# Moving small products to GpSimd and filling TensorE with unread products in a fused attention and gated-MLP kernel

## The chip, the core and the metric

The kernel runs on one core of one Trainium2 chip. A core has five engines that run at the same time and wait for one another by semaphores: TensorE (in the profile PE, with its weight loads as PEld), VectorE (DVE), ScalarE (ACT), GpSimd (POOL) and SyncE (SP). SBUF is the memory that all of them read; PSUM holds what TensorE writes, in eight banks of 128 x 512 fp32. The metric is the device time of one execution in microseconds.

## What is computed

The input x is 2048 positions by 512. Branch A is attention with 32 heads of width 16 that share one key and one value head; branch B is a gated MLP with a product over positions; a sigmoid gate mixes them.

```python
g = sigmoid((x * gate_w).sum(-1, keepdims=True))
# branch A: q has 32 heads, k and v have one
q, k, v = x @ wq, x @ wk, x @ wv
p = softmax(einsum('bhqd,bkd->bhqk', q, k) * Dh ** (-0.5))
a = einsum('bhqk,bkd->bhqd', p, v)  -> heads side by side -> @ wo
# branch B
z = gelu(x @ w_in);  z1 = z[..., :688];  z2 = layernorm(z[..., 688:])
b = (z1 * (w_sp @ z2 + b_sp)) @ w_out
out = g * a + (1 - g) * b
```

The softmax has 32 x 2048 x 2048 exponentials; they are the largest part of the work.

## The kernel before

All instructions of all engines are laid out by a Python program when the kernel is built. It keeps a clock for TensorE, ScalarE and VectorE, and for the engine whose clock is earliest it picks the ready candidate with the smallest priority number; each candidate carries an estimated length in nanoseconds. The estimates set only the order of the instructions on each engine; on the chip, semaphores set the times.

A **block** is 128 keys by 512 queries of one head. A **unit** is 64 such blocks: 16 key tiles for a group of four heads, which lie in the four quarters of the TensorE array. There are 32 units. Scores of a block are one matmul (32 rows of the array). ScalarE takes scores from two PSUM areas of three and two banks in turn and writes exponentials P; VectorE takes some blocks from bank 5 (BD) and builds the exponential as a polynomial, twice squared, in X, in batches of four blocks. How many blocks VectorE gets is decided by the clocks of the layout.

```python
BD = 5; BO = 6; BM = 7            # PSUM banks: VectorE's scores, attention sum, everything else
EB = ((0, 3), (3, 2))             # ScalarE's score areas
C512, C344 = 218.0, 148.0         # estimated lengths, ns
C4, C2 = 40 + 0.26 * 256 * DB, 30 + 0.5208 * 256 * DB     # DB = 4

def exp_op(k, n):                                          # L548, ScalarE
    op("act", lambda a: a.activation(P[:, k % NP, 0:512 * n], ps[:, 512 * b0:512 * (b0 + n)], ACT.Exp), ...)
def d_A(m, i):                                             # L572, VectorE, "dA"
    op("dve", lambda v: v.tensor_scalar(X[:, m % NX, 512 * i:512 * i + 512], bank(BD), PA, PB, ALU.mult, ALU.add), ...)
def d_poly(m):      # L580 square, L582 add a constant, L584 square; each on two halves of 1024
    ... v.tensor_tensor(x, x, x, ALU.mult)                 # estimate C2
    ... v.tensor_scalar(x, x, PC, None, ALU.add)           # estimate C4
    ... v.tensor_tensor(p_, x, x, ALU.mult)                # estimate C2
```

P and X are multiplied with V by quarter-array matmuls into bank 6 (BO); a column of ones in V gives the softmax sum. When a unit is done, VectorE normalises it and transposes it into OT for the output projection:

```python
def norm(pgx, u):
    ... v.transpose(T1[:], bank(BO))                                     # L594
    ... v.reciprocal(rc[:].unsqueeze(2), t1[:, :, 16:17])                # L595
    ... v.tensor_tensor(rcg[:], rc[:], RHO[:, c, :], ALU.mult)           # L597, RHO: the gate
    ... v.tensor_tensor(Tn[...], t1[:, :, 0:16], rr[:]..., ALU.mult)     # L598
    if jj == 1:                                                          # every second unit
        ... v.transpose(OT[:, c, jp, :], Tn[:, pr, :])                   # L602
```

Everything else of TensorE (projections of x to K, Q, V, z1, z2, the product over positions, the output) runs as "groups" through bank 7 (BM): a list of pieces, then an evacuation by VectorE. Between two pieces of a group other work may be put. The squares of Q, 16 instructions (L342), serve a bound on the scores. Such a group of pieces is that of V, 16 small matmuls, each a piece:

```python
return Group("V%d" % c, [(70, piece(k, dt)) for k in range(4) for dt in range(4)], [(150, e1), (100, e2), (130, e3)], ...)
```

Where TensorE has nothing ready in the next 100 ns, the layout may put an **unread product**: a full-array matmul of ones with ones, whose result nobody reads. It does so when the load of the last 3400 ns, in full matmuls of 512 columns, is below KEEP. An unread product goes to bank BM and only while no group is in it:

```python
def keep_pick(now):
    while load and load[0][0] < now - 3400:
        load.popleft()
    if sum(w_ for _, w_ in load) >= KEEP or misc["cur"] is not None or misc["free"] + LAT > now or tl_state[12] or st_["pu"] >= NU:
        return None
    ...
    return (now, 9, C512 + sw("M"), emit, None, "M")
```

`tl_state[12]` is set when the output tile 12 has begun to be built in BM ahead of the end.

In the trace all full-array matmuls carry line 277 and all quarter-array ones line 278, because one helper emits them.

Of the kernel before, what the change touches and what calls it, by code (L numbers as in the profile page):

```python
# [43 lines left out]
KEEP = 6.5  # L44
# [103 lines left out]
def build_kernel(nc, x_d, wq_d, wk_d, wv_d, wo_d, win_d, wsp_d, bsp_d, wout_d, gw_d, out_d):  # L148
    es = ExitStack()
    with es:  # L150
# [53 lines left out]
        s01 = sb("s01", [128, 2], F32)  # L204
        ct = sb("ct", [128, 3, NMAX * 32], F32)
# [11 lines left out]
        nhalf = sb("nhalf", [128, NST], F32)  # L217
        rstd = sb("rstd", [128, NST], F32)
# [14 lines left out]
        op("pool", lambda g: g.memset(nhalf[:], -0.5), w=["nhalf"])  # L233
        op("pool", lambda g: g.memset(bspz[:], 0.0), w=["bspz"])
# [57 lines left out]
        C4, C2 = 40 + 0.26 * 256 * DB, 30 + 0.5208 * 256 * DB  # L292
# [34 lines left out]
        def g_K(c):  # L327
            def done(t):
                T[("K", 0, c)] = t
                if c == 3:  # L330
                    k_shift()
                    T["K1"] = t + 8000
            return Group("K%d" % c, [(C512, lambda dt=dt: k_mm(c, dt, BM)) for dt in range(4)], [(620, lambda: k_ev(c, BM))],
                         lambda: when(("x", c)), done)
# [6 lines left out]
        def q_sq(qt):  # L341
            dve_q.append((350, lambda: op("dve", lambda v: v.tensor_tensor(sq[:, qt % 4, :], QA[:, qt % NQ, :], QA[:, qt % NQ, :], ALU.mult),  # L342
                                          r=[("Q", qt % NQ)], w=[("sq", qt % 4)], tag="sq"), T["now"] + 800, setT(("sq", qt))))

        def g_Q(qt):
            def done(t):
# [3 lines left out]
                         [(620, lambda: op("dve", lambda v: v.tensor_copy(QA[:, qt % NQ, :], bank(BM)), r=[BMK], w=[("Q", qt % NQ)], tag="Qev"))],  # L350
                         lambda: when(("x", qt // 4), "wq1", *([("Udone", 2 * (qt - NQ) + 1)] if qt >= NQ else [])), done)

        def g_N(c):
# [7 lines left out]
            return Group("N%d" % c, [(C512 if j == 0 else 60.0, piece(j)) for j in range(4)], [(620, ev)],  # L361
# [20 lines left out]
        def g_V(c):  # L382
# [17 lines left out]
            return Group("V%d" % c, [(70, piece(k, dt)) for k in range(4) for dt in range(4)], [(150, e1), (100, e2), (130, e3)],  # L400
# [14 lines left out]
        def g_MC():  # L415
# [17 lines left out]
            return Group("MC", pieces, [(1950, e1), (320, e2), (320, e3), (320, e4), (250, e5), (320, e6)],  # L433
                         lambda: when(("Kt", 2), ("Kt", 3), ("V", 2), ("V", 3)), setT("MC"))

        def g_R(c):
            def piece(dt):
                return lambda: mm(bank(BM), gw_rep[:, dt, :], xT[:, dt, 512 * c:512 * c + 512], dt == 0, dt == 3, ["gwr", ("x", c)], [BMK], tag="R")
            cr = ct[:, :, :].rearrange("p a n -> p (a n)")[:, 0:512]
            ev = lambda: op("dve", lambda v: v.transpose(cr, bank(BM)), r=[BMK], w=["ct0", "ct1"], tag="Rt")  # L440

            def done(t):
                def f():
                    op("act", lambda a: a.activation(RHO[:, c, :].unsqueeze(2), cr.rearrange("p (b w) -> p b w", w=32)[:, :, 0:1], ACT.Exp),
                       r=["ct0", "ct1"], w=[("RHO", c)], tag="rho")
                    T[("RHO", c)] = T["now"] + 500
                act_q.append((250, f, t))
            return Group("R%d" % c, [(C512, lambda dt=dt: piece(dt)()) for dt in range(4)], [(660, ev)],
                         lambda: when(("x", c), "MC", *([("RHO", c - 1)] if c else [])), done)

        def g_z1(ft, tc):
# [4 lines left out]
            return Group("z1", [(C512, piece(dt)) for dt in range(4)], [(620, ev)], lambda: when("win", ("x", tc)), setT(("z1", ft, tc)))  # L456

        def g_z2(st, h):
# [5 lines left out]
            return Group("z2", [(C344, piece(dt)) for dt in range(4)], [(440, ev)], lambda: when("win", ("x", st // 4)), setT(("z2", st, h)))  # L464

        def gelu_ops():
            out = []
            for k in range(4):
                def f(k=k):
# [3 lines left out]
                    for i in range(4):  # L473
                        st = 4 * k + i
                        for h in range(2):
                            dve_q.append((440, lambda st=st, h=h: op("dve", lambda v: v.bn_stats(bst[:, st, h, :], z2[:, FH * st + 344 * h:FH * st + 344 * h + 344]),  # L476
                                                                     r=[("z2", st)], w=[("bst", st)], tag="bn"), t, None))
                        dve_q.append((150, lambda st=st: op("dve", lambda v: v.bn_aggr(mv[:, st, :], bst[:, st, :, :]), r=[("bst", st)], w=["mv"], tag="bn"), t, None))
# [108 lines left out]
        def norm(pgx, u):  # L587
# [141 lines left out]
        def pe_pick(now):  # L729
# [414 lines left out]
        for u in range(NU):  # L1144
# [39 lines left out]
            for c_, f_, t_ in norm(ps2, u):  # L1184
                f_()
# [90 lines left out]
```

## Time and profile before

| | before |
|---|---|
| time, median of 3 runs | 856.54 us (855.01 to 858.22) |
| span of the profiled execution | 851.2 us |
| PE busy | 789.3 us, 5416 matmuls |
| DVE busy | 765.5 us |
| ACT busy | 776.0 us, of it 749.6 in 647 exponentials |
| POOL busy | 10.9 us, 17 instructions |
| mean granted TensorE clock | 0.927 |
| blocks of VectorE ("dA") | 432 of 2048 |
| unread products | 81 (12 of them ahead of the first work) |

Busy shares are averages over stages that are unlike: in the first 35 us the input arrives; from 280 to 320 us ScalarE computes the GELU and VectorE the layer norm; from 834 us on only the last tiles are left. The granted clock is that at which TensorE was allowed to run, 1.00 being full speed. A group's line gives count, busy time, the mean length of one, and the idle time of its engine just before it with what ended it. Lengths of neighbours on VectorE overlap a little, so a sum of lengths is more than the busy time.

### The profile page before, as it was taken

To read this page: it belongs to the slowest core of one execution; us is meant where nothing else is said; L and a number is where in the kernel's file an instruction comes from. 1 tells how busy PE (TensorE), PEld (TensorE's weight loads), DVE (VectorE), ACT (ScalarE), POOL (GpSimd) and SP (SyncE) were. 2 spreads that over 40 slices of the span, in tenths; PEclk is the share of its full clock that TensorE was granted. 3 is DMA by queue.
4 is the path that set the end of the run, shared out by engine and by line. 5 is a ranking of instruction groups with operands and counts; after the bars stand their busy time and mean duration, and the time that the engine had idled before them with its cause. 6 is when DMAs were issued, how large, how long until landed. Compare 5 with 4: busy or idle time off the path is not lost.

```text
span 851.2 us, 13946 instructions
## 1 busy us (share of the span) xinstructions
PE 789.3 (93%) x5416; PEld 209.9 (25%) x5416; DVE 765.5 (90%) x1471; ACT 776.0 (91%) x668; POOL 10.9 (1%) x17
## 2 busy tenths in 40 slices
PE   8899899999998879999999999999999999998886
PEld 2212222222222112222222222222222222222212
DVE  3579998899999899999999998999998999998981
ACT  5879997899999988999999999999998999999992
POOL 2000000000000010000000000000000000000000
PEclk8759996899999889999999999999998999999757
DMA  9700000000000000001300003100013000000000
GB/s 218 144 0 2 1 1 1 1 1 1 1 1 1 2 0 2 1 1 26 87 13 2 1 1 82 44 1 2 2 31 76 20 1 2 1 1 1 1 1 28
DMA packets 49050, 17.00 MB, mean 20 GB/s; under 512 B 44129, under 2 KB 48913, under 8 KB 48978
## 3 DMA queue, kind: packets, MB, share of 16 engines
q1 hardware_dynamic: 46210, 15.23, 8.0%
q10 hardware_dynamic: 2640, 0.56, 0.4%
q8 instruction: 44, 0.72, 0.4%
q0 software_dynamic: 128, 0.26, 0.2%
q14 instruction: 28, 0.23, 0.1%
HBM read 3.20 MB, written 2.10 MB: 6 GB/s over the span
## 4 chain that ended last, share of the span: by engine, by line
DVE 54%; PE 34%; issue 7%; ACT 3%; DMA 2%; SPq 0%; ACTq 0%
PE ps L278 22%; DVE X L572 20%; PE ps L277 12%; DVE X L580 9%; DVE X L584 7%; DVE X L582 5%; ACT P L548 2%; DVE T L594 2%; DVE bst L476 2%; DVE z L455 1%; DMA KA<-KA 1%; DVE Tn L598 1%; DVE z L462 1%; DMA xT<-in_A_x_dram 1%; DVE z L509 1%
## 5 line engine op out<-in xcount | busy, mean ns | idle before, releaser
L548 ACT ACTIVATE P<-ps 128x1536 bf16<-128x1536 f32 (+1 forms) x647 | 749.6, 1244 | 52.3 <-PE ps L278 48.1
L278 PE MATMUL ps<-QA,KA 32*128 32x512 bf16 x2048 | 364.1, 406 | 33.6 <-DVE X L572 16.4
L572 DVE TENSOR_SCALAR X<-ps 128x512 f16<-128x512 f32 x432 | 294.3, 681 | 39.4 <-PE ps L278 38.1
L278 PE MATMUL ps<-P,V 128*32 128x512 bf16 x1616 | 168.7, 412 | 0.0
L278 PEld LDWEIGHTS ps<-QA,KA 32*128 32x128 bf16 x2048 | 87.8, 91 | 326.4 <-ACT P L548 128.9
L584 DVE TENSOR_TENSOR X<-X 128x1024 bf16<-128x1024 f16 x216 | 144.1, 680 | 0.0
L580 DVE TENSOR_TENSOR X<-X 128x1024 f16<-128x1024 f16 x216 | 141.9, 680 | 0.0
L277 PE MATMUL ps<-wT,z 128*128 128x512 bf16 x384 | 118.6, 384 | 0.0
L582 DVE TENSOR_SCALAR X<-X 128x1024 f16<-128x1024 f16 x216 | 84.0, 415 | 0.0
L278 PE MATMUL ps<-X,V 128*32 128x512 bf16 x432 | 71.4, 407 | 0.1
L278 PEld LDWEIGHTS ps<-P,V 128*32 128x32 bf16 x1616 | 33.7, 95 | 61.3 <-issue 57.8
L277 PEld LDWEIGHTS ps<-wT,z 128*128 128x128 bf16 x384 | 29.3, 97 | 62.2 <-issue 52.7
L277 PE MATMUL ps<-ones 128*128 128x512 bf16 x81 | 32.4, 487 | 8.2 <-DVE bst L476 5.1
L277 PE MATMUL ps<-win,xT 128*128 128x344 bf16 x128 | 33.4, 339 | 3.9 <-DVE z L462 2.6
L277 PE MATMUL ps<-xT,win 128*128 128x512 bf16 x96 | 31.3, 386 | 2.6 <-DVE z L455 2.1
L277 PE MATMUL ps<-wout,z 128*128 128x512 bf16 x96 | 31.5, 400 | 1.8 <-DVE outsb L534 1.4
L594 DVE STREAM_TRANSPOSE T<-ps 128x512 f32<-128x512 f32 x32 | 22.6, 705 | 7.2 <-PE ps L278 7.2
L277 PE MATMUL ps<-xT,wq 128*128 128x512 bf16 x64 | 23.0, 414 | 0.3 <-DVE z L509 0.2
L278 PEld LDWEIGHTS ps<-X,V 128*32 128x32 bf16 x432 | 17.1, 95 | 19.8 <-issue 12.8
L277 PE MATMUL ps<-wo,OT 128*128 128x512 bf16 x64 | 20.5, 393 | 0.0
L462 DVE CAST z<-ps 128x344 bf16<-128x344 f32 x32 | 16.1, 504 | 2.0 <-PE ps L277 2.0
L277 PEld LDWEIGHTS ps<-win,xT 128*128 128x128 bf16 x128 | 10.1, 100 | 29.5 <-issue 12.9
(97 smaller groups left out, 293.3 us busy)
## 6 DMA issues: line engine op xcount, KB each, us to landing
out_dram<-outsb SPq DMA_DIRECT2D x16, 128.0 KB, 1.7
win<-in_B_w_in_dram SPq DMA_DIRECT2D x2, 688.0 KB, 5.5
wout<-in_B_w_out_dram SPq DMA_DIRECT2D x1, 640.0 KB, 9.0
wo<-in_A_wo_dram SPq DMA_DIRECT2D x1, 512.0 KB, 6.6
wq<-in_A_wq_dram ACTq DMA_DIRECT2D x1, 384.0 KB, 8.4
wT<-in_B_w_sp_dram SPq DMA_TRANSPOSE x16, 4.4
KA<-KA POOLq DMA_DIRECT2D x4, 64.0 KB, 2.5
wq<-in_A_wq_dram ACTq DMA_DIRECT2D x1, 128.0 KB, 3.9
```

The source lines that it names most:

```text
L277: return t.matmul(dst, lhsT, rhs, start=start, stop=stop)
L278: return t.matmul(dst, lhsT, rhs, start=start, stop=stop, tile_position=tp)
L455: ev = lambda: op("dve", lambda v: v.tensor_copy(z1[:, ft, 512 * tc:512 * tc + 512], bank(BM)), r=[BMK], w=[("z1", ft)], tag="z1ev")
L462: ev = lambda: op("dve", lambda v: v.tensor_copy(z2[:, FH * st + 344 * h:FH * st + 344 * h + 344], bank(BM, 344)), r=[BMK], w=[("z2", st)] ...
L476: dve_q.append((440, lambda st=st, h=h: op("dve", lambda v: v.bn_stats(bst[:, st, h, :], z2[:, FH * st + 344 * h:FH * st + 344 * h + 344]) ...
L509: ev = lambda: op("dve", lambda v: v.tensor_tensor(dst, ps[0:n, 512 * BM:512 * BM + 512], dst, ALU.mult), r=[BMK, ("z1", ft)], w=[("u", ft ...
L548: op("act", lambda a: a.activation(P[:, k % NP, 0:512 * n], ps[:, 512 * b0:512 * (b0 + n)], ACT.Exp), r=[("sc", k % 2)], w=[("P", k % NP)] ...
L572: op("dve", lambda v: v.tensor_scalar(X[:, m % NX, 512 * i:512 * i + 512], bank(BD), PA, PB, ALU.mult, ALU.add), r=[("bk", BD)], w=[("X", ...
L580: res.append((C2, lambda x=x, k=k: op("dve", lambda v: v.tensor_tensor(x, x, x, ALU.mult), r=[k], w=[k], tag="dU")))
L582: res.append((C4, lambda x=x, k=k: op("dve", lambda v: v.tensor_scalar(x, x, PC, None, ALU.add), r=[k], w=[k], tag="dV")))
L584: res.append((C2, lambda x=x, k=k, p_=p_, kp=kp: op("dve", lambda v: v.tensor_tensor(p_, x, x, ALU.mult), r=[k], w=[kp], tag="dW")))
L594: res = [(660, lambda: o("dve", lambda v: v.transpose(T1[:], bank(BO)), r=[("bk", BO)], w=["T1"], tag="T1"), setT(("O", u)))]
```

## The change

Several things are changed together:

- The reciprocal, the product with the gate and the scaling of each unit but the last go from VectorE to GpSimd. GpSimd builds the reciprocal as a power of -1. The second transpose on VectorE is planned 6 us after the unit's end.
- The squares of Q go to GpSimd.
- The 16 matmuls of a V group are one piece; the 14 of the MC group (sums over key tiles that correct for what the polynomial leaves out) are two. The gate's groups R get a buffer of their own (`cr`) and no longer wait for MC; R(0) is ahead of it.
- Unread products: KEEP is 7.5; below LOW = 6.0 they have priority 1.5, ahead of the products with V (2) and of groups (3), and need no idle time; they may use bank BD when VectorE has no block in it.
- The estimated lengths are replaced by others taken from measured lengths.

The diff, cut to its core (`...` marks cuts; declarations, the clean-up of the slow path's call and a few estimates of evacuations from 620 to 600 are left out):

```diff
@@ -41,7 +41,8 @@
-KEEP = 6.5
+KEEP = 7.5
+LOW = 6.0
 ...
@@ -231,6 +234,7 @@
+        op("pool", lambda g: g.memset(mone[:], -1.0), w=["mone"])
 ...
@@ -289,7 +293,7 @@
-        C4, C2 = 40 + 0.26 * 256 * DB, 30 + 0.5208 * 256 * DB
+        C4, C2 = 68 + 0.26 * 256 * DB, 68 + 0.5208 * 256 * DB
 ...
@@ -339,15 +343,16 @@
         def q_sq(qt):
-            dve_q.append((350, lambda: op("dve", lambda v: v.tensor_tensor(sq[:, qt % 4, :], QA[:, qt % NQ, :], QA[:, qt % NQ, :], ALU.mult),
-                                          r=[("Q", qt % NQ)], w=[("sq", qt % 4)], tag="sq"), T["now"] + 800, setT(("sq", qt))))
+            op("pool", lambda g: g.tensor_tensor(sq[:, qt % 4, :], QA[:, qt % NQ, :], QA[:, qt % NQ, :], ALU.mult),
+               r=[("Q", qt % NQ)], w=[("sq", qt % 4)], tag="sq")
+            T[("sq", qt)] = T["now"] + 5000
 ...
             return Group("Q%d" % qt, [(C512, lambda dt=dt: q_mm(qt, dt, BM)) for dt in range(4)],
-                         [(620, lambda: op("dve", lambda v: v.tensor_copy(QA[:, qt % NQ, :], bank(BM)), r=[BMK], w=[("Q", qt % NQ)], tag="Qev"))],
+                         [(600, lambda: op("dve", lambda v: v.tensor_copy(QA[:, qt % NQ, :], bank(BM)), r=[BMK], w=[("Q", qt % NQ)], tag="Qev"))],
 ...
@@ -397,7 +402,11 @@
-            return Group("V%d" % c, [(70, piece(k, dt)) for k in range(4) for dt in range(4)], [(150, e1), (100, e2), (130, e3)],
+            def all_():
+                for k in range(4):
+                    for dt in range(4):
+                        piece(k, dt)()
+            return Group("V%d" % c, [(480, all_)], [(150, e1), (100, e2), (130, e3)],
 ...
@@ -430,30 +439,32 @@
             e6 = lambda: op("dve", lambda v: v.scalar_tensor_tensor(cc, cc, s01[:, 0:1], ct[:, 1, :], ALU.mult, ALU.add), r=["CC", "ct1", "s01"], w=["CC"], tag="CC")
-            return Group("MC", pieces, [(1950, e1), (320, e2), (320, e3), (320, e4), (250, e5), (320, e6)],
+            def some(h):
+                for c_, f_ in pieces[NMAX * h:NMAX * h + NMAX]:
+                    f_()
+            return Group("MC", [(500, lambda: some(0)), (500, lambda: some(1))], [(1950, e1), (320, e2), (320, e3), (320, e4), (250, e5), (320, e6)],
 ...
                 return lambda: mm(bank(BM), gw_rep[:, dt, :], xT[:, dt, 512 * c:512 * c + 512], dt == 0, dt == 3, ["gwr", ("x", c)], [BMK], tag="R")
-            cr = ct[:, :, :].rearrange("p a n -> p (a n)")[:, 0:512]
-            ev = lambda: op("dve", lambda v: v.transpose(cr, bank(BM)), r=[BMK], w=["ct0", "ct1"], tag="Rt")
+            ev = lambda: op("dve", lambda v: v.transpose(cr[:], bank(BM)), r=[BMK], w=["cr"], tag="Rt")
 ...
                 def f():
-                    op("act", lambda a: a.activation(RHO[:, c, :].unsqueeze(2), cr.rearrange("p (b w) -> p b w", w=32)[:, :, 0:1], ACT.Exp),
-                       r=["ct0", "ct1"], w=[("RHO", c)], tag="rho")
+                    op("act", lambda a: a.activation(RHO[:, c, :].unsqueeze(2), cr[:, :].rearrange("p (b w) -> p b w", w=32)[:, :, 0:1], ACT.Exp),
+                       r=["cr"], w=[("RHO", c)], tag="rho")
 ...
             return Group("R%d" % c, [(C512, lambda dt=dt: piece(dt)()) for dt in range(4)], [(660, ev)],
-                         lambda: when(("x", c), "MC", *([("RHO", c - 1)] if c else [])), done)
+                         lambda: when(("x", c), *([("RHO", c - 1)] if c else [])), done)
 ...
             ev = lambda: op("dve", lambda v: v.tensor_copy(z1[:, ft, 512 * tc:512 * tc + 512], bank(BM)), r=[BMK], w=[("z1", ft)], tag="z1ev")
-            return Group("z1", [(C512, piece(dt)) for dt in range(4)], [(620, ev)], lambda: when("win", ("x", tc)), setT(("z1", ft, tc)))
+            return Group("z1", [(C512, piece(dt)) for dt in range(4)], [(600, ev)], lambda: when("win", ("x", tc)), setT(("z1", ft, tc)))
 ...
@@ -473,9 +484,9 @@
-                            dve_q.append((440, lambda st=st, h=h: op("dve", lambda v: v.bn_stats(bst[:, st, h, :], z2[:, FH * st + 344 * h:FH * st + 344 * h + 344]),
+                            dve_q.append((520, lambda st=st, h=h: op("dve", lambda v: v.bn_stats(bst[:, st, h, :], z2[:, FH * st + 344 * h:FH * st + 344 * h + 344]),
 ...
-                        dve_q.append((150, lambda st=st: op("dve", lambda v: v.bn_aggr(mv[:, st, :], bst[:, st, :, :]), r=[("bst", st)], w=["mv"], tag="bn"), t, None))
+                        dve_q.append((135, lambda st=st: op("dve", lambda v: v.bn_aggr(mv[:, st, :], bst[:, st, :, :]), r=[("bst", st)], w=["mv"], tag="bn"), t, None))
 ...
@@ -588,19 +599,45 @@
-            fast = pgx is pg
 ...
-            rr = rcg if fast else rc
-            res = [(660, lambda: o("dve", lambda v: v.transpose(T1[:], bank(BO)), r=[("bk", BO)], w=["T1"], tag="T1"), setT(("O", u)))]
-            res.append((210, lambda: o("dve", lambda v: v.reciprocal(rc[:].unsqueeze(2), t1[:, :, 16:17]), r=["T1"], w=["rc"], tag="rc"), None))
-            if fast:
-                res.append((110, lambda: o("dve", lambda v: v.tensor_tensor(rcg[:], rc[:], RHO[:, c, :], ALU.mult), r=["rc", ("RHO", c)], w=["rcg"], tag="rcg"), None))
-            res.append((380, lambda: o("dve", lambda v: v.tensor_tensor(
-                Tn[:, pr, :].rearrange("p (b w) -> p b w", w=32)[:, :, 16 * jj:16 * jj + 16],
-                t1[:, :, 0:16], rr[:].unsqueeze(2).broadcast_to([128, 16, 16]), ALU.mult), r=["T1", "rcg" if fast else "rc"], w=[("Tn", pr, jj)], tag="Tn"), None))
-            if jj == 1:
-                res.append((650, lambda: o("dve", lambda v: v.transpose(OT[:, c, jp, :], Tn[:, pr, :]), r=[("Tn", pr, 0), ("Tn", pr, 1)], w=[("OT", c, jp)], tag="T2"),
-                            setT(("OT", c, jp))))
+            lsum = t1[:, :, 16:17]
+            tn = Tn[:, pr, :].rearrange("p (b w) -> p b w", w=32)[:, :, 16 * jj:16 * jj + 16]
+
+            def f_t1():
+                o("dve", lambda v: v.transpose(T1[:], bank(BO)), r=[("bk", BO)], w=["T1"], tag="T1")
+
+            def f_rc(e):
+                if e == "dve":
+                    o("dve", lambda v: v.reciprocal(rc[:].unsqueeze(2), lsum), r=["T1"], w=["rc"], tag="rc")
+                else:
+                    o("pool", lambda g: g.tensor_tensor(rc[:].unsqueeze(2), lsum, mone[:].unsqueeze(2), ALU.pow), r=["T1", "mone"], w=["rc"], tag="rc")
+
+            def f_rcg(e):
+                o(e, lambda v: v.tensor_tensor(rcg[:], rc[:], RHO[:, c, :], ALU.mult), r=["rc", ("RHO", c)], w=["rcg"], tag="rcg")
+
+            def f_tn(e, s_, k):
+                o(e, lambda v: v.tensor_tensor(tn, t1[:, :, 0:16], s_[:].unsqueeze(2).broadcast_to([128, 16, 16]), ALU.mult), r=["T1", k], w=[("Tn", pr, jj)], tag="Tn")
+
+            def f_t2():
+                o("dve", lambda v: v.transpose(OT[:, c, jp, :], Tn[:, pr, :]), r=[("Tn", pr, 0), ("Tn", pr, 1)], w=[("OT", c, jp)], tag="T2")
+
+            if pgx is not pg:
+                return [f_t1, lambda: f_rc("dve"), lambda: f_tn("dve", rc, "rc")] + ([f_t2] if jj else [])
+            res = []
+            if u < NU - 1:
+                def f_all():
+                    f_t1()
+                    f_rc("pool")
+                    f_rcg("pool")
+                    f_tn("pool", rcg, "rcg")
+                res.append((716, f_all, setT(("O", u)), 0.0))
+            else:
+                res.append((716, f_t1, setT(("O", u)), 0.0))
+                res.append((281, lambda: f_rc("dve"), None, 0.0))
+                res.append((205, lambda: f_rcg("dve"), None, 0.0))
+                res.append((387, lambda: f_tn("dve", rcg, "rcg"), None, 0.0))
+            if jj:
+                res.append((633, f_t2, setT(("OT", c, jp)), 6000.0 if u < NU - 1 else 0.0))
 ...
@@ -636,7 +673,7 @@
-        first = deque([g_V(0), g_K(1), g_K(2), g_V(1), g_K(3), g_V(2), g_V(3), g_MC(), g_R(0), g_Q(1), g_R(1), g_R(2), g_R(3)])
+        first = deque([g_V(0), g_K(1), g_K(2), g_V(1), g_K(3), g_V(2), g_V(3), g_R(0), g_MC(), g_Q(1), g_R(1), g_R(2), g_R(3)])
 ...
@@ -884,9 +921,12 @@
             if not cands or min(c[0] for c in cands) > now + 100:
-                tl = tail_pick(now) or keep_pick(now)
+                tl = tail_pick(now)
 ...
                     cands.append(tl)
+            kp = keep_pick(now)
+            if kp and (kp[1] < 9 or not cands or min(c[0] for c in cands) > now + 100):
+                cands.append(kp)
 ...
@@ -897,13 +937,20 @@
                 load.popleft()
-            if sum(w_ for _, w_ in load) >= KEEP or misc["cur"] is not None or misc["free"] + LAT > now or tl_state[12] or st_["pu"] >= NU:
+            have = sum(w_ for _, w_ in load)
+            if have >= KEEP or st_["pu"] >= NU:
+                return None
+            if misc["cur"] is None and misc["free"] + LAT <= now and not tl_state[12]:
+                b = BM
+            elif dbank["blk"] is None and dbank["free"] + LAT <= now and not tl_state[13]:
+                b = BD
+            else:
 ...
                 after = [pg.ops["dve"][-1]] if gel_on and gel else []
-                mm(bank(BM), ones[:, 0:128], ones[:], True, True, ["ones"], [BMK], tag="keep", after=after)
-            return (now, 9, C512 + sw("M"), emit, None, "M")
+                mm(bank(b), ones[:, 0:128], ones[:], True, True, ["ones"], [("bk", b)], tag="keep", after=after)
+            return (now, 1.5 if have < LOW else 9, C512 + sw("M"), emit, None, "M")
 ...
@@ -938,8 +985,8 @@
-                for z, (c_, f_, d_) in enumerate(norm(pg, u)):
-                    norm_q.append((c_, f_, (lambda u=u: when(("RHO", u // 8))) if z == 2 else t_end + LAT, d_))
+                for c_, f_, d_, w_ in norm(pg, u):
+                    norm_q.append((c_, f_, lambda w_=w_: None if when(("RHO", u // 8)) is None else t_end + LAT + w_, d_))
 ...
@@ -997,7 +1044,7 @@
-                    cands.append((t, 1, 94 + 426.7 * len(bl), e2, f2))
+                    cands.append((t, 1, (0, 510, 940, 1346)[len(bl)], e2, f2))
 ...
@@ -1033,7 +1080,7 @@
-                cands.append((dbank["ready"], 3, 600, e1, f1))
+                cands.append((dbank["ready"], 3, 601, e1, f1))
 ...
```

More of the change, by code (lines that the diff above doesn't have):

```diff
@@ L204, in build_kernel @@
         s01 = sb("s01", [128, 2], F32)
+        cr = sb("cr", [128, 512], F32)
         ct = sb("ct", [128, 3, NMAX * 32], F32)
@@ L217, in build_kernel @@
         nhalf = sb("nhalf", [128, NST], F32)
+        mone = sb("mone", [128, NST], F32)
         rstd = sb("rstd", [128, NST], F32)
@@ L332, in done @@
                     T["K1"] = t + 8000
-            return Group("K%d" % c, [(C512, lambda dt=dt: k_mm(c, dt, BM)) for dt in range(4)], [(620, lambda: k_ev(c, BM))],
+            return Group("K%d" % c, [(C512, lambda dt=dt: k_mm(c, dt, BM)) for dt in range(4)], [(600, lambda: k_ev(c, BM))],
                          lambda: when(("x", c)), done)
@@ L360, in done @@
                     bad_ops(t)
-            return Group("N%d" % c, [(C512 if j == 0 else 60.0, piece(j)) for j in range(4)], [(620, ev)],
+            return Group("N%d" % c, [(C512 if j == 0 else 60.0, piece(j)) for j in range(4)], [(600, ev)],
                          lambda: when(*[("sq", 4 * c + j) for j in range(4)]), done)
@@ L463, in g_z2 @@
                             r=[BMK], w=[("z2", st)], tag="z2ev")
-            return Group("z2", [(C344, piece(dt)) for dt in range(4)], [(440, ev)], lambda: when("win", ("x", st // 4)), setT(("z2", st, h)))
+            return Group("z2", [(C344, piece(dt)) for dt in range(4)], [(428, ev)], lambda: when("win", ("x", st // 4)), setT(("z2", st, h)))
         def gelu_ops():
@@ L1183, in build_kernel @@
                         kt == 0, kt == 15, ["P"], [("bk", BO)], (0, 32 * g))
-            for c_, f_, t_ in norm(ps2, u):
+            for f_ in norm(ps2, u):
                 f_()
```

## Prediction

> **What bounds the kernel now.** I read the page's first two parts first. Three engines are almost equally full, so no single busy share names the bound:
>
> ```profile
> PE 789.3 (93%) x5416; PEld 209.9 (25%) x5416; DVE 765.5 (90%) x1471; ACT 776.0 (91%) x668; POOL 10.9 (1%) x17
> ...
> PEclk8759996899999889999999999999998999999757
> ```
>
> GpSimd (POOL) is empty. The row of granted clocks, one digit for each 21 us, has dips: near 40, 140, 290, 640 and 800 us. So I cut the span into stretches (columns: time, length, then busy us of PE, PEld, DVE, ACT, POOL with instruction counts, granted clock, DMA share, GB/s):
>
> ```profile
> 35.00:62.00 27.00, 25.60 (x131) 5.27 (x123) 17.53 (x36) 18.22 (x17) 0.15 (x1) 0.51 0.17 30
> ...
> 133.00:156.00 23.00, 22.93 (x116) 4.30 (x116) 16.96 (x30) 15.89 (x14) 0.00 (x0) 0.50 0.00 1
> 160.00:260.00 100.00, 92.97 (x673) 25.70 (x674) 99.07 (x188) 96.63 (x84) 0.00 (x0) 1.00 0.00 1
> ...
> 660.00:760.00 100.00, 97.88 (x716) 26.57 (x708) 96.90 (x185) 97.04 (x85) 0.00 (x0) 1.00 0.02 5
> 797.00:838.00 41.00, 35.24 (x215) 7.02 (x212) 30.63 (x58) 34.02 (x31) 0.00 (x0) 0.56 0.00 1
> ```
>
> Two regimes are to be seen. At clock 1.00 VectorE (DVE) is 97 to 99% busy and ScalarE (ACT) 97%: these two share the exponentials, and together they set the pace. At clock 0.50 TensorE is never idle and both others fall to about 70%: TensorE sets the pace.
>
> The pace can be counted. [...]ScalarE takes 5 blocks in two exponentials, VectorE one in each "dA". In the stretch 660 to 760 us the groups by line say:
>
> ```profile
> L548 ACT ACTIVATE P<-ps 128x1024 bf16<-128x1024 f32 x85 | 97.9, 1242 | 3.0 <-PE ps L278 2.8
> ...
> L572 DVE TENSOR_SCALAR X<-ps 128x512 f16<-128x512 f32 x59 | 40.1, 680 | 1.9 <-PE ps L278 1.9
> ```
>
> That is 85 x 2.5 + 59 = 271 blocks in 100 us, 2.71 per us. The same counts give 47 blocks in 35 to 62 us (16 exponentials, 7 dA: 1.74 per us), 46 in 133 to 156 us (14 and 11: 2.00), 50 in 640 to 660 us (16 and 10: 2.50), and 95.5 in 797 to 834.5 us, where ScalarE ends (31 and 18: 2.55). Against 2.71 the lost time is 9.7 + 6.0 + 1.5 + 2.2 = 19.4 us.
>
> Why the clock falls there: I counted full-array matmuls (line 277) and quarter-array ones (line 278, four at once) per 3.4 us. For line 277 alone:
>
> ```profile
> 122.40:125.80 3.40, 1.11 (x5) 1.00 0.00 0
> ...
> 129.20:132.60 3.40, 0.01 (x1) 1.00 0.00 0
> 132.60:136.00 3.40, 0.79 (x2) 0.58 0.00 0
> ...
> 156.40:159.80 3.40, 1.41 (x6) 0.90 0.00 0
> ```
>
> With line 278 (26, 21, 15 and 17 matmuls, a quarter each) the load is 11.5, then 6.3 and 5.8, then 10.3 full matmuls per 3.4 us. The clock goes to half behind the two low ones and comes back behind the high one. From 799 to 833 us there is almost no line-277 work, the load is 3.8 to 6.8, and the clock stays at 0.50 but for one short return.
>
> [...] The trace before shows one overlap, the single power that GpSimd computes, and the two-input squares of line 584 and 580 at its side:
>
> ```profile
> 308.32 2.93 POOL L482 TENSOR_TENSOR rstd<-ve,nhalf 128x16 f32<-128x16 f32 x1 [273.17 <-DVE ve L481]
> ...
> 308.75 0.68 DVE L584 TENSOR_TENSOR X<-X 128x1024 bf16<-128x1024 f16 x1
> ...
> 310.68 0.68 DVE L580 TENSOR_TENSOR X<-X 128x1024 f16<-128x1024 f16 x1
> ```
>
> [...] No GpSimd product is in this trace. [...]
>
> **Part by part.**
>
> *Normaliser and squares off VectorE.* Of each of 31 units VectorE loses the reciprocal (250 ns), the product with the gate (174) and the scaling (424); some 75 ns of each lies under its neighbour (two squares of 680 take 1.28 us in the timeline, so each starts 0.60 after the other). That is 31 x (0.848 - 0.22) = 19.5 us at least and 31 x 0.848 = 26.3 at most, in a chain of waiting small instructions nearer the latter: 25. The 16 squares of Q (400 ns each, 0.33 net) are 5. Together 30 us off VectorE.
>
> [...] Net 21 us.
>
> What is 21 us on VectorE worth? One block costs VectorE 0.60 + (4 x 0.60 + 2 x 0.33)/4 = 1.37 us and ScalarE 0.46 (12 alternating exponentials, 30 blocks, ran 13.87 us). Freed VectorE time is shared out by moving blocks: 21 x 0.46/(0.46 + 1.37) = 5.3 us, about 11 more blocks on VectorE. It counts only where these two set the pace, three quarters of the span: **-4 us**.
>
> *Order from measured lengths.* The order of all instructions is fixed beforehand from lengths in the source. Before, a square counted as 563 ns and the addition as 306; the trace spaces them 600 and 330. A batch of four blocks was short by 4 x 37 + 2 x 24 = about 0.2 us, 108 batches 22 us: the plan gave VectorE more than it could do, and in 160 to 260 us VectorE is at 99% while TensorE waits for it. The new numbers (601, 334, and 940/1346 for the exponentials, 2.29 a pair against 2.31 measured) repair that. ScalarE waited 52 us in all for TensorE, of which only about 20 lie at full clock. I take a fifth: **-4 us**.
>
> *Unread products.* KEEP rises from 6.5 to 7.5 units of load, below 6.0 they get priority over all but the scores, and they may use bank BD too. That is aimed at 133 to 156 us (bank BM was taken by a projection group) and at 797 to 834 us (BM was taken by the early output tile). V in one run and the two-piece MC group shorten the first hole; part of that hole is the key copy and the MC products, which remain. BD is often taken by VectorE's blocks. So I take half of 19.4: **-10 us**.
>
> *Price of the above.* The 81 products become perhaps 200. At full clock each takes 0.22 us, 0.32 with a switch; 120 x 0.32 = 38 us, mostly in TensorE's gaps, but each may hold the next scores up by 0.1 to 0.2 us where ScalarE has little queued. Four V runs hold scores up by a microsecond each. **+2 us**.
>
> Sum: 856.5 - 4 - 4 - 10 + 2 = **840.5 us**, 1.9% less.
>
> **Rivals.** [...] (b) *TensorE becomes the bound at full clock.* It is already 98% busy in 660 to 760 us; if 120 or more products each delay scores by 0.2 us that ScalarE feels, +20 us cancel everything: about 860. Against it: busy here includes pipeline tails, and ScalarE's wait for TensorE in that stretch is only 2.8 us. (c) *The half clock vanishes but for the start, and the plan fits:* -17, -7, -6, +2 gives 828.
>
> **Range and chances.** 826 to 855: the lower end is (c), the upper end is (a) with little clock gained. 2% faster is 839.4, almost at my centre, so faster by over 2%: 0.47; within 2%: 0.46; slower by over 2% needs rival (b) in full: 0.07.
>
> **What would show it.** Right: the clock of 133 to 156 and of 797 to 834 us at or near 1.00, mean 0.95 or more instead of 0.927; VectorE near its old busy time with 440 or more dA instead of 432; POOL about 140 us; squares of lines 580 and 584 still 680 ns. Wrong: those squares clearly longer in the mean (a); ScalarE's wait for TensorE above 52 us with 300 or more unread products (b); a wait of the second transpose for GpSimd; or the dips of the clock still in place.

## The result, and the profile after

The changed kernel takes 816.14 us (median of 4 runs, 809.48 to 818.43) against 855.77 us before: a ratio of 0.954, 95% interval 0.945 to 0.964. That is 40 us less, where 16 were predicted and 30 was the end of the range. Here and below a ratio compares executions of one round without those over 1.5% above the fastest of their kernel, so it can differ by some 1% from that of the medians, and where too few are left none is given.

From the page of the changed kernel, the engines' totals and the granted clock:

```profile
PE 762.3 (93%) x5443; PEld 205.8 (25%) x5443; DVE 748.7 (92%) x1372; ACT 765.0 (94%) x666; POOL 151.5 (19%) x127
...
PEclk9798799979999899999999999999999999999967
```

No engine got much emptier; the span closed around them. The mean clock is 0.959 instead of 0.927. Taking it as either full or half, an estimate from these means, half clock lasted 2 x 0.041 x 816 = 67 us instead of 2 x 0.073 x 851 = 124 us.

The stretches of the changed kernel, with the columns of the prediction (time, length, busy us of PE, PEld, DVE, ACT, POOL, then clock and DMA):

```profile
35.00:62.00 27.00, 25.22 (x165) 6.14 (x164) 23.45 (x43) 23.96 (x24) 5.17 (x4) 0.87 0.15 32
133.00:156.00 23.00, 21.87 (x180) 6.40 (x175) 23.00 (x44) 22.58 (x21) 3.94 (x3) 1.00 0.00 1
...
660.00:760.00 100.00, 96.29 (x706) 26.05 (x705) 95.97 (x172) 98.71 (x87) 22.45 (x17) 1.00 0.01 4
780.00:805.00 25.00, 21.97 (x117) 4.58 (x117) 16.23 (x29) 15.37 (x14) 0.96 (x3) 0.53 0.00 1
```

The old dips of the clock at 35 to 62 and 133 to 156 us are shallow (0.87 for 0.51) or gone (1.00 for 0.50). New ones stand at 78 to 90 us (0.50) and 176 to 184 us (0.50), and the one at the end is still there (0.53). At full clock ScalarE is nearly full: 98.7 of 100 us, 87 exponentials where 85 stood, and 60 blocks of VectorE where 59 stood.

Two groups of GpSimd's new work (count, busy us and mean ns of one, then its idle time before them), and below them the lines of VectorE's polynomial, beside which that work runs:

```profile
L613 POOL TENSOR_TENSOR rc<-T,mone 128x16 f32<-128x16 f32 x31 | 91.0, 2934 | 556.4 <-DVE T L607 556.4
L619 POOL TENSOR_TENSOR Tn<-T,rcg 128x256 bf16<-128x256 f32 x31 | 20.4, 660 | 2.4
```

```profile
L595 DVE TENSOR_TENSOR X<-X 128x1024 bf16<-128x1024 f16 x218 | 148.8, 694 | 0.0
L591 DVE TENSOR_TENSOR X<-X 128x1024 f16<-128x1024 f16 x218 | 146.1, 686 | 0.0
...
L593 DVE TENSOR_SCALAR X<-X 128x1024 f16<-128x1024 f16 x218 | 90.5, 439 | 0.0
```

The squares became 14 and 6 ns longer (680 before), the addition 24 (415 before). Times 218 each that is 9.6 us. In out_pool below, without GpSimd's new work, they take 682 and 417 ns. The means hide how uneven this is: only 31 of the 654 are longer by more than 30 ns. Those met a product of GpSimd, as here (start, us):

```profile
172.09 1.04 POOL L346 TENSOR_TENSOR sq<-QA 128x512 bf16<-128x512 bf16 x1
172.16 1.52 DVE L595 TENSOR_TENSOR X<-X 128x1024 bf16<-128x1024 f16 x1
```

The squares that met only the power (L613), 28 of L591 and 21 of L595, took 673 and 676 ns on the mean, and those that met nothing of GpSimd 678, so the power made them no longer. The changed kernel has 108 unread products, and VectorE has 436 blocks.

### The profile page after: what moved, and what is told of

Same layout as the page of the kernel before. It is cut to its first block, busy times and chain, and to the rows that moved or that the text cites. A ratio compares the mean times of both kernels' runs of the same rounds, so it can differ in the third digit from the quotient of the medians.

```text
span 815.8 us, 14110 instructions
## 1 busy us (share of the span) xinstructions
PE 762.3 (93%) x5443; PEld 205.8 (25%) x5443; DVE 748.7 (92%) x1372; ACT 765.0 (94%) x666; POOL 151.5 (19%) x127
## 4 chain that ended last, share of the span: by engine, by line
DVE 38%; PE 35%; ACT 14%; issue 12%; DMA 1%; SPq 0%; ACTq 0%; DVEq 0%
PE ps L282 22%; DVE X L583 15%; ACT P L559 13%; PE ps L281 13%; DVE X L591 6%; DVE X L595 5%; DVE X L593 4%; DVE bst L487 2%; DVE z L466 2%; DMA xT<-in_A_x_dram 1%; DVE T L607 1%; DVE z L473 1%; DVE z L497 1%; DVE z L520 1%; DVE QA L355 1%
## 5 line engine op out<-in xcount | busy, mean ns | idle before, releaser
L559 ACT ACTIVATE P<-ps 128x1536 bf16<-128x1536 f32 (+1 forms) x645 | 738.8, 1276 | 29.1 <-PE ps L282 27.5
L282 PE MATMUL ps<-QA,KA 32*128 32x512 bf16 x2048 | 344.0, 395 | 29.8 <-ACT P L559 15.7
L613 POOL TENSOR_TENSOR rc<-T,mone 128x16 f32<-128x16 f32 x31 | 91.0, 2934 | 556.4 <-DVE T L607 556.4
L282 PE MATMUL ps<-P,V 128*32 128x512 bf16 x1612 | 163.8, 398 | 0.6 <-DVE T L607 0.5
L595 DVE TENSOR_TENSOR X<-X 128x1024 bf16<-128x1024 f16 x218 | 148.8, 694 | 0.0
L591 DVE TENSOR_TENSOR X<-X 128x1024 f16<-128x1024 f16 x218 | 146.1, 686 | 0.0
L593 DVE TENSOR_SCALAR X<-X 128x1024 f16<-128x1024 f16 x218 | 90.5, 439 | 0.0
L282 PE MATMUL ps<-X,V 128*32 128x512 bf16 x436 | 76.9, 395 | 0.3 <-DVE X L595 0.3
L281 PE MATMUL ps<-ones 128*128 128x512 bf16 x108 | 37.6, 437 | 9.6 <-DVE bst L487 3.4
L346 POOL TENSOR_TENSOR sq<-QA 128x512 bf16<-128x512 bf16 x16 | 18.7, 1172 | 20.5 <-DVE QA L355 17.1
```

Of the source, the lines that this page charges most:

```text
L281: return t.matmul(dst, lhsT, rhs, start=start, stop=stop)
L282: return t.matmul(dst, lhsT, rhs, start=start, stop=stop, tile_position=tp)
L346: op("pool", lambda g: g.tensor_tensor(sq[:, qt % 4, :], QA[:, qt % NQ, :], QA[:, qt % NQ, :], ALU.mult), r=[("Q", qt % NQ)], w=[("sq", qt ...
L591: res.append((C2, lambda x=x, k=k: op("dve", lambda v: v.tensor_tensor(x, x, x, ALU.mult), r=[k], w=[k], tag="dU")))
L593: res.append((C4, lambda x=x, k=k: op("dve", lambda v: v.tensor_scalar(x, x, PC, None, ALU.add), r=[k], w=[k], tag="dV")))
L595: res.append((C2, lambda x=x, k=k, p_=p_, kp=kp: op("dve", lambda v: v.tensor_tensor(p_, x, x, ALU.mult), r=[k], w=[kp], tag="dW")))
```

## The experiments

The change has four parts, each of which can be done alone or undone: **lengths**, **GpSimd** (normaliser and squares of Q), **groups** (V, MC, the gate), and the **rule** for unread products. I set three theories side by side. Theory 1 is the prediction's: the clock is the largest term, the rest is small. Theory 2: the order made from better lengths is the largest. Theory 3: VectorE's time is worth more than I reckoned. Below, "before" is the kernel before, run on the same chip beside the others. Times are medians.

### One part alone

**in_lengths**: the estimated lengths replaced, nothing else; those of the normaliser's steps belong to the part GpSimd.

```diff
-C4, C2 = 40 + 0.26 * 256 * DB, 30 + 0.5208 * 256 * DB
+C4, C2 = 68 + 0.26 * 256 * DB, 68 + 0.5208 * 256 * DB
-cands.append((t, 1, 94 + 426.7 * len(bl), e2, f2))
+cands.append((t, 1, (0, 510, 940, 1346)[len(bl)], e2, f2))
 ... (and the small ones: 620 to 600, 440 to 428, 440 to 520, 150 to 135, 600 to 601)
```

> The kernel before with only the estimated lengths replaced. The plan then gives VectorE 416 blocks instead of 432. Theory 1 (the sizes of the prediction: clock first, the rest small): about 4 us less than before, 0.995. Theory 2 (a plan nearer to the chip is the largest part, because a late VectorE holds TensorE's fixed order up everywhere): 12 us less or more, 0.985 or below, with ScalarE's wait for TensorE at full clock down. Theory 3 (the worth of VectorE's time is the largest part): no gain, 1.00, since VectorE has as much other work as before.

Measured: 819.6 us against 857.5, ratio 0.949 (0.940 to 0.959). **These numbers alone bring about as much as the whole change.** They change only the order, the sharing of blocks and, by the same rule, the count of unread products (68 instead of 81). Theory 2 holds.

**in_pool**: only the work for GpSimd.

```diff
-op("dve", ... reciprocal, product with RHO, scaling; squares of Q)
+op("pool", ...)      # with the old lengths everywhere else
```

> The kernel before with only the normaliser's small products and the squares of Q on GpSimd, old lengths. The plan gives VectorE 436 blocks instead of 432. Theory 1: about 4 us less, 0.995. Theory 2: under 5 us less, since the plan still believes VectorE faster than it is. Theory 3: 12 us less or more, 0.985 or below; VectorE's late work shrinks by 30 us whatever the plan.

Measured: 838.5 us, ratio 0.974 (0.965 to 0.982): some 19 us less by medians, far more than my 4. The edit also brings the measured lengths of the unit's transposes (716 and 633 ns for 660 and 650) and the delay of the second one; these are not tested apart.

**in_keep**: only the new rule for unread products.

```diff
-KEEP = 6.5
+KEEP = 7.5; LOW = 6.0   # priority 1.5 below LOW, bank BD allowed
```

> The kernel before with only the new rule for unread products: 125 of them instead of 81. Theory 1: about 10 us less, 0.988, mean clock 0.95 or above. Theories 2 and 3: under 6 us less, and the clock explains it all: pace at full clock stays 2.7 blocks per us.

Measured: 839.5 us, ratio 0.975 (0.966 to 0.983), clock 0.953 to 0.963 over its runs where before has 0.902 to 0.939. Some 18 us less by medians, while the pace at full clock stays: 86 exponentials and 55 first steps from 660 to 760 us are 270 blocks, where 271 stood. On the old lengths Theory 1 is right about this part, but for its size.

**in_groups**: only V in one run, MC in two pieces, the gate's own buffer and place.

```diff
-Group("V%d" % c, [(70, piece(k, dt)) for k in range(4) for dt in range(4)], ...)
+Group("V%d" % c, [(480, all_)], ...)
 ... (likewise MC; cr a tile of its own; R(0) ahead of MC)
```

> The kernel before with only V in one run, the MC group in two pieces, a buffer of its own for the gate and the new order of the first groups. Theory 1: 2 to 4 us less, all before 62 us, since the first hole of the clock closes. Theories 2 and 3: about the same, within 3 us.

Measured: 850.5 us, ratio 0.986 (0.976 to 0.995): 7 us less by medians, more than any theory had.

Taken alone, the four bring 38 + 19 + 18 + 7 = 82 us by medians; together 40. So they overlap: what one part brings, another has in part brought already.

### One part undone

**out_lengths** (old lengths in the changed kernel), **out_pool** (the small products back on VectorE), **out_keep** (old rule), **out_groups** (old groups): each edit is the one above, the other way round.

> The changed kernel with the old estimated lengths. Theory 1: 4 us more than the changed kernel, about 820 if that is 816. Theory 2: 12 us more or above, 828 to 835. Theory 3: about the same, within 3 us.

Measured: 839.5 us, ratio to before 0.979 (0.970 to 0.987). Without the lengths 23 of the 40 us are lost.

> The changed kernel with the normaliser and the squares of Q back on VectorE. The plan gives VectorE 416 blocks instead of 436. Theory 1: 4 us more than the changed kernel. Theory 2: under 6 us more, since the plan knows VectorE's load and shares the blocks out anew. Theory 3: 12 us more or above.

Measured: 820.8 us, ratio 0.955 (0.944 to 0.966): 5 us above the changed kernel by medians, but with the same ratio (0.954 there). With right lengths GpSimd's help lies between nothing and 5 us; my 4 fits, but no gain is shown.

> The changed kernel with the old rule for unread products: 78 of them instead of 108. Theory 1: about 10 us more than the changed kernel, mean clock back near 0.93. Theories 2 and 3: under 6 us more.

Measured: 807.6 us, ratio 0.942 (0.933 to 0.951): **less** than the changed kernel, and the clock stays at 0.955 to 0.961. No theory had that.

> The changed kernel with the old groups of V, MC and the gate. Theory 1: 2 to 4 us more, all before 62 us. Theories 2 and 3: within 3 us.

Measured: 816.3 us, ratio 0.953 (0.943 to 0.962): no loss that can be seen here.

### What in the lengths does it

**in_poly**: only the first pair of lines of in_lengths (the polynomial's steps). **in_exp**: only the second pair (the exponentials).

> The kernel before with only the lengths of the polynomial's steps corrected (square 563 to 601 ns, addition 306 to 334). The plan gives VectorE 420 blocks. If it is VectorE's underrated length that delays TensorE's fixed order, this brings most of what all lengths brought (858 to 820): 830 or less. If it is ScalarE's overrated length, little: 850 or more.

Measured: 833.1 us (819.2 to 837.8) against 853.8, between the two bands; its four runs scatter too much for an interval.

> The kernel before with only the lengths of the exponentials corrected (947 to 940 ns for two blocks, 1374 to 1346 for three). The plan gives VectorE 420 blocks. If VectorE's underrated length is the cause: 850 or more. If ScalarE's overrated length is (the plan brings the next scores too late for ScalarE): 830 or less.

Measured: 828.4 us against 853.8, ratio 0.980 (0.960 to 0.999). Each half alone brings more than half of the 38 us by medians, so neither of the two single causes that I had set against each other is the only one. Both errors push one way: VectorE rated too quick, ScalarE too slow.

**in_cap**: old lengths, but per unit no more blocks for VectorE than in_lengths gives it (416 in all).

```diff
+CAP = [1, 2, 4, 3, 3, 4, 3, 3, 3, 4, 3, 3, 3, 4, 3, 4, 3, 3, 3, 4, 3, 3, 4, 3, 3, 4, 3, 3, 4, 3, 3, 5]
+if (64 - un["hi"]) // 4 >= CAP[u]:
+    continue
```

> The kernel before with its old lengths, but each unit may give VectorE only as many blocks as the corrected lengths give it: 416 instead of 432. If the number of blocks is the cause (VectorE was simply given too much): about 820, like all lengths corrected. If the order is (when each instruction stands in TensorE's queue against its neighbours): 845 or more.

Measured: 856.4 us (843.6 to 874.2) against 853.8: nothing gained. **The smaller number of blocks alone does not do it; what is left is the order.** Whether the number helps beside right lengths is not shown.

**in_long**: right lengths, but the polynomial overrated by as much as it was underrated.

```diff
-C4, C2 = 68 + 0.26 * 256 * DB, 68 + 0.5208 * 256 * DB
+C4, C2 = 96 + 0.26 * 256 * DB, 106 + 0.5208 * 256 * DB
```

> The kernel before with all lengths corrected, but the polynomial's steps overrated by as much as they were underrated (square 639 ns, addition 362). The plan gives VectorE 428 blocks. If only a late VectorE hurts (TensorE waits for it in order), this is as good as the corrected lengths, about 820. If any error of the plan hurts alike, it is near the kernel before, 845 or more.

Measured: 844.4 us, ratio 0.992 (0.988 to 0.996). An error the other way loses most of the gain.

Each of these is one plan, and every edit shifts the whole order, so chance is a rival for any single one. Over all kernels it is not: the nine with the measured lengths take 804 to 821 us, the six with old ones 838 us or more, whatever else they have. For the half corrections and for in_long chance is not ruled out.

The views of the waits show what goes with it. First the kernel before (engine, line, whom it waited for: us in all, times, longest us); L548 is the exponential, L572 VectorE's first step:

```profile
PEld ps L278 <- ACT P L548: 128.9, 292, 2.0
PEld ps L278 <- DVE X L572: 85.1, 216, 1.2
ACT P L548 <- PE ps L278: 48.1, 88, 3.9
```

Then in_lengths:

```profile
PEld ps L278 <- ACT P L548: 178.7, 430, 1.1
PEld ps L278 <- DVE X L572: 54.8, 163, 1.2
...
ACT P L548 <- PE ps L278: 26.7, 33, 4.5
```

My account was this: TensorE works in the order of the plan; where the plan thought VectorE would be done, and it is not, TensorE stands before VectorE's next scores (85 us), and ScalarE's scores, next in the queue, stand with it (ScalarE waits 48 us). With right lengths TensorE waits for ScalarE instead, which is as it should be when ScalarE is full. in_exp does not fit the middle of this:

```profile
PEld ps L278 <- DVE X L572: 78.7, 200, 1.3
...
ACT P L548 <- PE ps L278: 25.6, 56, 2.8
```

ScalarE's wait is halved there, though TensorE waits for VectorE nearly as long as before. So it is shown that a better order takes away ScalarE's waits for TensorE, but not that TensorE's stand before VectorE is the path. Most of what goes lies outside the start and the end. From 62 to 760 us, before and then in_lengths:

```profile
ACT P L548 <- PE ps L278: 31.9, 68, 3.9
```

```profile
ACT P L548 <- PE ps L278: 9.0, 18, 1.4
```

In in_cap the old picture is nearly back, with fewer blocks (L549 and L573 are the same two lines there):

```profile
PEld ps L279 <- DVE X L573: 76.9, 191, 1.2
...
ACT P L549 <- PE ps L279: 48.4, 82, 4.1
```

The overrated plan fails in another way. ScalarE's timeline in in_long (start, us, instruction, and in brackets the idle time before it):

```profile
150.45 4.62 ACT L548 ACTIVATE P<-ps 128x1536 bf16<-128x1536 f32 x4 [5.16 <-PE ps L278]
...
184.05 22.96 ACT L548 ACTIVATE P<-ps 128x1024 bf16<-128x1024 f32 x20 [9.76 <-PE ps L278]
...
213.95 21.63 ACT L548 ACTIVATE P<-ps 128x1024 bf16<-128x1024 f32 x19 [6.94 <-PE ps L278]
...
242.31 6.17 ACT L548 ACTIVATE P<-ps 128x1536 bf16<-128x1536 f32 x5 [6.73 <-PE ps L278]
```

With one more of 4.17 us these long waits are 33 us. Before the one at 184 us stand:

```profile
182.40 0.39 PE L278 MATMUL ps<-X,V 128*32 128x512 bf16 x2 [0.44 <-DVE X L584]
...
182.87 0.70 DVE L594 STREAM_TRANSPOSE T<-ps 128x512 f32<-128x512 f32 x1
...
183.62 0.55 PEld L278 LDWEIGHTS ps<-P,V 128*32 128x32 bf16 x16 [0.47 <-DVE T L594]
```

The unit's last products are those of VectorE's blocks, and they wait for its last squares. Only then can VectorE take the sum out of its bank (L594), and only then can the products of P with V of the next unit begin; none had run since 168.7 us. ScalarE starts 0.4 us after them. Its scores had been written, so by this order of events it lacked a free buffer for P. All five holes have this sequence: VectorE finishes the unit late, and ScalarE, ahead in the next one, stands. From 320 to 760 us, away from such holes, in_long has the best pace of the old-rule kernels on VectorE's old work: 387 x 2.5 + 250 = 1217.5 blocks, against 1200 in in_lengths, 1168.5 in in_cap and 1172.5 before. So what the overrated plan costs lies in a few places, and what the underrated one costs is spread over the whole stretch.

### Why the other parts add so little, and one of them harms

Four kernels on one chip. **after_again** is the changed kernel; **old_rule_again** has the old rule for unread products; **keep_low0** has the new rule without its priority (`LOW = 0.0`); **len_pool** has only lengths and GpSimd.

> The changed kernel itself, to stand on one chip beside the next three. If the new rule for unread products costs time once the lengths are right, this is the slowest of the four with groups and GpSimd work changed: some 8 us above the old rule. If the earlier difference (816 against 808) was chance, the two are within 3 us.

Measured: 814.3 us (811.4 to 819.1), ratio to before 0.963 (0.950 to 0.976).

> The changed kernel with the old rule for unread products (78 instead of 108), run once more beside the changed kernel. If the new rule costs time: about 808 against 816. If not: the same within 3 us.

Measured: 803.9 us (802.2 to 806.1), ratio 0.948 (0.937 to 0.960). Its slowest run is faster than the changed kernel's fastest: the new rule costs 10 us, as in out_keep.

> The changed kernel with LOW = 0: KEEP 7.5 and the second bank stay, but no unread product is ever put ahead of work that is ready (102 instead of 108). If it is their priority that costs time: as good as the old rule, about 808. If it is their number or bank BD: like the changed kernel, about 816.

Measured: 812.7 us (809.3 to 816.5). Priority is not the reason.

> The kernel before with the measured lengths and the GpSimd work alone; old groups, old rule for unread products (75). If lengths and GpSimd work are all that helps: at or below the changed kernel, 806 to 816. If the new groups carry some of it: 4 us or more above the old-rule kernel.

Measured: 817.4 us (814.4 to 824.7). Beside lengths, GpSimd and the old rule the new groups are worth 817.4 - 803.9 = 13 us, though under the new rule (out_groups) they showed nothing. Read the other way, the new rule costs 10 us beside the new groups only: with the old ones it is 816.3 (out_groups) against 817.4 us, on two chips.

Then the rule's two other pieces. **keep_bm** keeps threshold and priority and leaves out the bank; **keep_65** keeps the bank and leaves out threshold and priority.

```diff
-            elif dbank["blk"] is None and dbank["free"] + LAT <= now and not tl_state[13]:
-                b = BD                                    # keep_bm
-KEEP = 7.5; LOW = 6.0
+KEEP = 6.5; LOW = 0.0                                     # keep_65
```

> The changed kernel with KEEP 7.5 and LOW 6.0, but unread products in bank BM only (95 instead of 108). If bank BD is what costs time (an unread product there stands between VectorE's reading and its next scores): 804 to 808. If the number or the threshold is: 812 to 816.

Measured: 804.2 us (802.1 to 808.4), ratio 0.940 (0.934 to 0.946).

> The changed kernel with the old threshold 6.5 and no priority, but bank BD allowed (89 instead of 108; the old rule had 78). If bank BD is what costs time: 812 to 816. If the threshold of 7.5 is: 804 to 808.

Measured: 815.0 us (812.7 to 818.3), ratio 0.952 (0.945 to 0.958). **The second bank is what costs the 10 us**: the changed kernel in both its runs, keep_low0 and keep_65 have it and lie at 813 to 816 us; out_keep, old_rule_again and keep_bm do without and lie at 804 to 808. These are three plans with it and two without, all with the new groups.

The time is lost early. From 62 to 320 us the first trace of the changed kernel has 193 exponentials and 133 first steps, 193 x 2.5 + 133 = 615.5 blocks; keep_bm has 204 and 136, or 646. At 2.8 blocks per us that is 11 us. But this trace is the worst of its kind: after_again and keep_low0 have 632, keep_65 636.5, and without the bank old_rule_again has 652 and out_keep 653.5, so the gap is 3 to 14 us. From 320 to 760 us the changed kernel and keep_bm are equal, at 1222 and 1221.5. ScalarE's timeline in keep_bm has this stretch in it,

```profile
80.60 145.74 ACT L559 ACTIVATE P<-ps 128x1536 bf16<-128x1536 f32 x128 [0.88 <-PE ps L282]
```

128 exponentials without a gap of note; after_again has one of 3.36 us at 195 us there, with the sequence of in_long's: the sum is taken out until 194.90 us, the products of P with V begin at 195.08, ScalarE at 195.53. TensorE's waits of its full-array line for VectorE's first step, after_again and then keep_bm:

```profile
PEld ps L281 <- DVE X L583: 9.1, 14, 1.3
...
PE ps L281 <- DVE X L583: 2.3, 5, 0.8
```

```profile
PEld ps L281 <- DVE X L583: 4.5, 10, 1.1
...
PE ps L281 <- DVE X L583: 0.5, 1, 0.5
```

An unread product in BD must wait until VectorE has read that bank; these waits, in which all full-array matmuls are counted, are 11.4 against 5.0 us. They do not explain the 10 us: keep_65 has only 5.5 us of them and is as slow. What is left is that the products in BD shift all that the plan lays after them; by which step is not shown.

keep_bm and old_rule_again, at 804 us, beat both kernels of the change.

## Why the prediction was wrong, point by point

- **The failed step: "Order from measured lengths", -4 us.** Measured alone it is -38 us (in_lengths). I had found the error of the plan and its sign, and had worked out its size, 22 us over the span. Then I valued it by ScalarE's visible idle time ("ScalarE waited 52 us in all for TensorE, of which only about 20 lie at full clock. I take a fifth"; 52.3 us is all its idle time, 48.1 of it for TensorE). The fraction was wrong: from 62 to 760 us, mostly at full clock, the wait fell from 31.9 to 9.0 us, by 23 us and not by 4. The idle time is also not all of the waiting: from 320 to 760 us before, 367 exponentials fill 422.6 us, 2.30 us a pair; after, 384 fill 436.5 us, 2.27 a pair, and the page shows both as busy. And the clock was left out: in_lengths lifts it as well. At one clock on one chip, 0.940 and 0.939, in_lengths takes 824.3 us against 844.4: of its 38 us some 20 are pace and the rest goes with the clock. What lifts the clock there is not shown.
- **The clock.** "Unread products, -10 us" is too small for what they do on the old lengths (-18 us, in_keep), and in the whole change they are not what brings the gain. One kernel's own runs give an estimate of the exchange: the kernel before ran 840.3 us at clock 0.946 and 862.0 at 0.910, so 22 us for 2 x 0.036 x 851 = 61 us more of half clock, about a third. The 57 us less of half clock are then worth some 20 us. But in_lengths has clocks of 0.940 to 0.968 with fewer unread products than before (68), and out_keep 0.955 to 0.961 with 78. One reading of mine was also wrong: the clock does not come back behind the stretch of 10.3 full matmuls. The line of 156.40 to 159.80 us has a mean of 0.90, so the clock, half before and full after, was back about 0.7 us into it; the stretch before, with 3 and 22 matmuls at 0.50, has 8.5 in the same count.
- **GpSimd, -4 us**: not contradicted where the lengths are right (0 to 5 us, out_pool), and 19 us on the old ones. A likely reading, not shown, is that there it takes away work that the plan had underrated (reciprocal 210 against 250 ns, gate product 110 against 174), and so part of the same error. The -4 counts 21 of the 30 us taken off VectorE; what lies between is my estimate of what GpSimd's products cost VectorE beside them, which no run had shown. In the changed kernel the squares and the addition are longer by 9.6 us in all. Nor had a run shown the 140 us of GpSimd's busy time: it is 151.5, with 2.93 us for a power and 0.33, 0.66 and 1.17 us for the products of 16, 256 and 512 elements.
- **The price of unread products, +2 us**: I expected 200 of them, there are 108, and yet the rule costs 10 us beside the new groups, with bank BD and hardly through TensorE's time. Threshold and priority without the bank (keep_bm) cost nothing.
- **Rival (a), VectorE's squares clearly longer beside GpSimd's work, and (b), TensorE as the bound,** did not come. The upper end of the range, 855, stood on (a), and no run showed what that takes: the squares are 1 to 2% longer on the mean (686 and 694 ns for 680), and single ones that meet a product of GpSimd take up to 1.52 us, but of 654 squares and additions only 31 are longer by more than 30 ns. ScalarE's wait for TensorE fell from 48.1 to 27.5 us. Rival (c) had the right direction, but took the lengths at -6 us, so its 828 was too high.
- **The clock "of 797 to 834 us at or near 1.00"**: wrong; near the new end, from 780 to 805 us, it is 0.53. That of 133 to 156 us came, at 1.00.
- "VectorE [...] with 440 or more dA": 436. The second transpose does not wait for GpSimd: none of VectorE's waits in the changed kernel is for it.

## What to carry to other kernels

Where one engine serves two others from a queue in fixed order, the estimated lengths that make the order are worth tuning first: corrections, most of them of 1 to 9%, were worth 4% of the time here, and in the one plan tried with an error in the other direction most of that was lost. Value such an error by all the waits of the busiest engine that a better order can take away, and by the clock, not by a cautious fraction of its idle time. A filler instruction is not free because its engine is idle: ask which buffer it needs, and who is still reading it.

## What the runs showed of the hardware that I had not expected

GpSimd needs 2.93 us for a power of 16 elements per partition, but only 0.33 us for a product of 16, 0.66 us for 256 (fp32) and 1.17 us for 512 (bf16). Beside the products single squares of VectorE took up to 1.52 us for 0.68; beside the power they took 673 and 676 ns on the mean, and 678 with nothing of GpSimd beside them. Over all, the squares grew by 1 to 2% (680 to 686 and 694 ns) and the addition by 6% (415 to 439). For the exponential, a longer record did not mean a slower engine here: with less idle time before it (3.5 us in all for 17.4, from 320 to 760 us) its mean rose from 1458 to 1491 ns for three blocks, while the spacing of a pair fell from 2.30 to 2.27 us.
